# Decode attention with a token mixer: mixer tiles that go on without a pause, one activation for a half's exponentials, V alternating with the next K

## Chip, cores, metric

One core of one Trainium2 chip runs one program. The metric is the device time of one execution in microseconds, the median of three runs; lower is better.

## What is computed

Two inputs of one token (512 channels) go through attention over a long cache, a token mixer, attention again with the same cache and weights, and the mixer again. Each step adds to its input and starts with a layer norm.

```python
def A(x, k_cache, v_cache, wq, wo):            # 32 query heads, 8 heads of K and V, 32768 keys of 128
    q = split_heads(x @ wq)                    # B=2, 32, 1, 128
    scores = q @ repeat(k_cache, 4).T * 128 ** -0.5
    return (softmax(scores) @ repeat(v_cache, 4)).merge_heads() @ wo

def M(x, w1, b1, w2, b2):                      # one token, F=1792
    u = gelu(layernorm(x)[b, s, d] * w1[s, f] + b1[f])      # b, d, f
    return (u @ w2 + b2)                       # b, s, d

x = x + A(layernorm(x)); x = x + M(layernorm(x)); x = x + A(layernorm(x)); x = x + M(layernorm(x))
```

All numbers are float32. K and V of one head and one input are 16 MB each.

## The kernel before

The work is cut into 32 *units*: a layer, an input b and a head of K and V. `units` (L188 on) lists them: the first layer's twelve units of the six "passing" heads, then the ones of heads 5 and 7, in which the layers are interleaved so that one input's mixer runs while the other input still streams its cache. Unit 13 is the last of input 0 in the first layer (`N1`), unit 16 that of input 1 (`N2`), unit 18 is `N3`. Unit 14 and unit 17 are the ones "between layers": while their K chunks are streamed, the mixer of unit 13's (16's) input is computed, and the q of unit 15 (18) needs that mixer's result. Head 7 is the "keeper": of unit 13's and 16's K and V some chunks stay in SBUF and are used again by units 15 and 18. Of K those are chunks 2, 4 and 5 (`KEPT_K`).

A unit has 8 chunks of K and 8 of V, of 2 MB. `stream` lists all chunks with a sort key; the final loop walks it, issues a load on SP's queue (`load_k`, `load_v`) and records the chunk's matmuls (`k_chunk`, L307, 16 matmuls of 128x512 into the PSUM tile `scores`; `v_chunk`, L417, 16 into `acc`). `t` counts chunks. Loads of the other units take up to 8 MB; from unit 14's third K chunk to unit 18 they take 2 MB, into a ring of three buffers (`RING`): a load waits for the chunk that was in its buffer. All other work hangs on that count: `at(t, f, ...)` puts `f` behind the t-th chunk; within one count, lower `rank` comes first, then the order of the `at` calls. Engines run their instructions in the order in which they were recorded.

For a unit the steps are: `make_q` in three parts (two of the projection, L250, one of turning the row into a column, L262); `max_1` and `max_2` (the maximum over all scores, through DVE and PE, to `neg`, L337); `turn_scores` (a DVE transpose from PSUM into S0 or S1, one half of the chunks each); `exponentials` (four activations with an accumulated sum for each half, L346); `denominators`; after the last V chunk `out_1`, `out_2`. The mixer is `mix_1`, `mix_2` (layer norm to `slope` and `shift`), 14 times `hidden_tile` (a gelu activation of 128x512, L640) and `hidden_out` (its matmul, L629), then `take_rows`, `mix_4`, `to_columns`. Between layers its tiles lie in S0, S1 and one tile `hid`, which are free until the unit's scores are turned into S0 and S1; `BURSTS` says how many tiles are made at each count from `begin` on:

```python
BURSTS = (3, 3, 3, 3, 0, 1, 1)
when = [(begin + k, place) for k, m in enumerate(BURSTS) for place in (*S, None)[-m:] if m]
for f, (w, place) in enumerate(when):
    at(w + 1, hidden_out, key, f, rank=0)
    at(w, hidden_tile, key, f, place, rank=2)
```

So three tiles are made behind a K chunk and multiplied behind the next one, four times over; then come the exponentials of unit 14 (17), and the last two tiles follow, one behind each of the first two V chunks. The V chunks 0 to 5 of unit 14 (17) follow one another, and then K of unit 15 (18) and V take turns: the key of V chunk c is `(n + 1) * NCH - 0.5 + max(c / (2 * NCH) - 0.5, c - ASIDE + 1)`, with `ASIDE = 6`.

Of the kernel before, what the change touches and what calls it, by code (L numbers as in the profile page):

```python
# [9 lines left out]
AF = mybir.ActivationFunctionType  # L10
ALU = mybir.AluOpType
AX = mybir.AxisListType

P = 128
# [10 lines left out]
KEPT_K = {2: 9, 4: 7, 5: 8}  # L25
KEPT = {1: (8, 6), 3: (8, 11), 4: (3, 13), 5: (8, 3), 6: (8, 4), 7: (8, 5)}
REST = 3
ASIDE = 6
BURSTS = (3, 3, 3, 3, 0, 1, 1)
KEPT_Q = 4  # L30
RESIDENT = (5, 7)
PIECES = (32, 16, 8, 4, 4)
# [8 lines left out]
def gqa_mixer_kernel(ctx: ExitStack, tc: tile.TileContext, x, kt, v, wqo, cols, out):  # L41
# [17 lines left out]
    nc = tc.nc  # L59
# [3 lines left out]
    NCH = kt.shape[1] // (CK * DH)  # L63
    HKV = U // B
    R = wqo.shape[2] // (2 * D)
    DT = D // P
    FT = (cols.shape[1] - 1) // 3
# [3 lines left out]
    HALVES = NCH // PACK  # L71
    SCALE = DH ** -0.5
# [88 lines left out]
    S = [const.tile([P, 512], F32, name=f"S{k}") for k in range(HALVES)]  # L161
# [34 lines left out]
    N3 = len(units) - 1  # L196
# [9 lines left out]
    def row_tile():  # L206

        return S[HALVES - 1]
# [16 lines left out]
    def unit_of(n):  # L225

        return units[n]
# [47 lines left out]
    sc_ps, mx, lsum, oT = {}, {}, {}, {}  # L275
# [55 lines left out]
    neg = {}  # L331
# [11 lines left out]
    def exponentials(n, half):  # L343
        s = S[half].rearrange("p (t h) -> p t h", h=R)
        for h in range(R):
            nc.scalar.activation(  # L346
                s[:, :, h],
                s[:, :, h],
                AF.Exp,
                bias=neg[n][:, h : h + 1],  # L350
                scale=SCALE,
                accum_out=lsum[n][:, half, h : h + 1],
            )

    def stays(n, c):
# [327 lines left out]
    for n in range(NU):  # L683
        stream += [(n * NCH + c + m - 1, 0, n, c, m, limit) for c, m, limit in parts(n, 0)]
        for c, m, limit in parts(n, 1):
            if n in (N1, N2):
                key = (n + 1) * NCH + 1 + (c + 1) / (2 * NCH)
            elif n in (N1 + 1, N2 + 1):
                key = (n + 1) * NCH - 0.5 + max(c / (2 * NCH) - 0.5, c - ASIDE + 1)
            else:  # L690
                key = (n + 1) * NCH + c + m - 1 + (LAG if N1 < n <= N3 else 0)
# [4 lines left out]
    kbeg, k_done, vbeg, v_done, t = {}, {}, {}, {}, 0  # L696
# [7 lines left out]
    def at(time, f, *a, rank=1):  # L704
        done.setdefault(time, []).append((rank, f, a))
# [5 lines left out]
    for n in range(NU):  # L711
        layer, b, h = unit_of(n)
        kend, vend = k_done[n, NCH - 1], v_done[n, NCH - 1]
        ahead = v_done[n - 1, NCH - 1] if n else 0
        urgent = n in (N1, N2, NU - 1)
        if n:
            if n in (N1 + 2, N2 + 2):
                q0 = q1 = mixed[layer - 1, b]
            else:
                q0 = kbeg[n] - 6  # L720
                q1 = q0 + 1
            q2 = q1 + 1
            assert q2 <= kbeg[n]
            at(q0, make_q, n, 0)
            at(q1, make_q, n, 1)
            at(q2, make_q, n, 2)
        if n and (units[n] == (0, 0, h) or h in passing and units[n] == (1, 0, h)):
            at(kbeg[n] - 10, load_weights, h, (again if layer else weight_cell)[h])
        if n in (N1 + 1, N2 + 1):
            t1 = kend  # L730
            at(kend, max_1, n, 0)
            at(kend, max_2, n)
            at(kend, exponentials, n, 0)
        else:
            t1 = max(kend + 2, ahead + (2 if urgent else 4))
            at(kend + 1, max_1, n)
            at(kend + 2, max_2, n)
            at(max(k_done[n, HC - 1], v_done[n - 1, HC - 1] if n else 0), turn_scores, n, 0)
            at(kend + 2, exponentials, n, 0)
        at(t1, turn_scores, n, 1)  # L740
        at(t1, exponentials, n, 1)
        at(t1 + (1 if n == NU - 1 else 2), denominators, n)
        if n == NU - 1:
            at(t1 + 1, gelu_table)
            at(t1 + 1, last_rows, (layer, b))
            at(vend, last_out, n)
            at(vend, last_mixer, n)
            continue
        assert vbeg[n + 1] >= vend and (n + 2 >= NU or vbeg[n + 1] > vend)
        at(min(vend + 1, vbeg[n + 1]), out_1, n)  # L750
        change = n in (N1, N2)
        at(vend + (1 if change else 2), out_2, n)
        if units[n] == lay[layer, b][-1]:
            key = (layer, b)
            begin = vend + (2 if change else 3)
            at(vend, mix_1, key)
            at(begin - 1, take_rows, key, row_tile())
            at(begin, mix_2, key)
            at(vend + 1, gelu_table)
            if change:  # L760
                assert vend + 5 < k_done[n + 1, NCH - 1] == begin + 4 and sum(BURSTS) == FT
                when = [(begin + k, place) for k, m in enumerate(BURSTS) for place in (*S, None)[-m:] if m]
                e = begin + len(BURSTS)
            else:

                exps = [k_done[m, NCH - 1] + 2 for m in (n + 1, n + 2)]
                exps += [max(e, v_done[m, NCH - 1] + 4) for e, m in zip(exps, (n, n + 1))]
                when = [(w, None) for w in range(begin, begin + FT + 1 + len(exps)) if w not in exps][: FT + 1]
                e = when.pop()[0]

            for f, (w, place) in enumerate(when):
                at(w + 1, hidden_out, key, f, rank=0)
                at(w, hidden_tile, key, f, place, rank=2)
            at(e, take_rows, key, None, rank=2)
            at(e + 1, mix_4, key)
            if layer + 1 < LAYERS:
                at(e + 2, to_columns, key)
                mixed[key] = e + 2
# [9 lines left out]
    t = 0  # L788
# [62 lines left out]
```

## Time and profile before

| | |
|---|---|
| time, median of 3 runs | 2511.01 us (2510.29 to 2512.43) |
| time of the profiled execution | 2509.4 us |
| its span, first to last instruction | 2507.6 us |
| granted TensorE clock, mean | 0.77 |
| busy: PE, DVE, ACT | 55%, 8%, 8% of the span |
| read from HBM | 1068.00 MB, 426 GB/s over the span |

The profile is of one execution. In its tables the engines are PE (TensorE matmul), PEld (its weight load), DVE (VectorE), ACT (ScalarE), POOL (GpSimd) and SP (SyncE, which issues the loads); L417 is line 417 of the kernel. A row of the timeline has start, duration, engine, line, operation, tiles, count, and in brackets the idle time before it with what ended that. A row of busy time by stretch has, for each engine, busy time and number of instructions, then the granted TensorE clock, the share of the 16 DMA engines that was busy, and GB/s.

### The profile page before, as it was taken

The page shows a single profiled execution, that of the slowest core. Times are in us where ns is not written, and L with a number is a line of the kernel's source. Part 1 is how long each engine was busy: PE and PEld are TensorE (multiplying, and loading weights), DVE is VectorE, ACT ScalarE, POOL GpSimd, SP SyncE. Part 2 cuts the span into 40 slices and gives each one's busy share as a digit, 9 for nine tenths or more (in the row PEclk, how much of TensorE's full clock was granted, in tenths as well). Part 3 has the DMA queues.
Part 4 walks back from the last instruction along what each step waited for, and adds up shares of the span by engine and source line. Part 5 has one row for each costly group of instructions (what it writes and reads, how often), then busy time and mean ns, then how long its engine had stood idle before and what let it go on. Part 6 is the DMA issues. An engine that isn't in the chain of part 4 may idle for free.

```text
span 2507.6 us, 20418 instructions
## 1 busy us (share of the span) xinstructions
PE 1382.3 (55%) x9302; PEld 365.0 (15%) x9302; DVE 207.2 (8%) x587; ACT 197.3 (8%) x582; POOL 4.9 (0%) x17
## 2 busy tenths in 40 slices
PE   4545554545445554666676766454546555455546
PEld 1111111111111111111111211111111111111112
DVE  1000000000000000001101100000000000010002
ACT  0000000000000000002012010000000000011102
POOL 0000000000000000000000000000000000000000
PEclk8777777777777777878897987777778777777778
DMA  9999999999999999999999999999999999999996
GB/s 419 433 433 431 433 434 432 433 429 434 433 433 433 431 426 433 424 427 418 427 427 428 408 428 434 433 432 434 431 432 430 433 434 432 431 432 432 430 433 282
DMA packets 31200, 1069.32 MB, mean 426 GB/s; under 512 B 3717, under 2 KB 3721, under 8 KB 4362
## 3 DMA queue, kind: packets, MB, share of 16 engines
q1 hardware_dynamic: 30824, 1067.99, 99.0%
q8 instruction: 73, 1.20, 0.2%
q14 instruction: 13, 0.11, 0.0%
q10 hardware_dynamic: 290, 0.03, 0.0%
HBM read 1068.00 MB, written 0.00 MB: 426 GB/s over the span
## 4 chain that ended last, share of the span: by engine, by line
DMA 74%; PE 25%; ACT 0%; DVE 0%; issue 0%; ACTq 0%; SPq 0%; DVEq 0%
DMA mem<-in_kt_dram 37%; DMA mem<-in_v_dram 37%; PE acc L417 11%; PE scores L307 11%; PE misc L250 1%; PE rows L461 0%; PE misc L454 0%; PE rows L629 0%; PE misc L335 0%; ACT S L346 0%; ACT mem L614 0%; PE misc L446 0%; PE misc L215 0%; PE misc L262 0%; PE misc L327 0%
## 5 line engine op out<-in xcount | busy, mean ns | idle before, releaser
L307 PE MATMUL scores<-mem,qpad 128*32 128x512 f32 x4096 | 616.4, 721 | 594.3 <-DMA mem<-in_kt_dram 593.6
L417 PE MATMUL acc<-mem,S 128*16 128x512 f32 x4088 | 618.3, 743 | 481.0 <-DMA mem<-in_v_dram 473.6
L346 ACT ACTIVATE S<-S,neg 128x128 f32<-128x128 f32 x256 | 132.3, 521 | 2080.0 <-DVE neg L337 1603.8
L307 PEld LDWEIGHTS scores<-mem,qpad 128*32 128x32 f32 x4096 | 142.3, 127 | 981.3 <-DMA mem<-in_kt_dram 525.1
L417 PEld LDWEIGHTS acc<-mem,S 128*16 128x16 f32 x4088 | 134.8, 111 | 850.7 <-issue 697.9
L317 DVE TENSOR_REDUCE mx<-scores 128x1 f32<-128x512 f32 x64 | 44.3, 692 | 854.3 <-PE scores L307 854.3
L250 PE MATMUL misc<-mem,xnT 128*2 128x512 f32 (+1 forms) x144 | 69.6, 611 | 2.8 <-issue 1.8
L341 DVE STREAM_TRANSPOSE S<-scores 128x512 f32<-128x512 f32 x64 | 45.5, 711 | 143.9 <-PE acc L417 143.2
L346 ACT ACTIVATION_READ_ACCUMULATOR S<-S,neg 128x1 f32 x256 | 47.9, 187 | 0.0
L461 PE MATMUL rows<-mem,oT 128*1 128x512 f32 x248 | 33.8, 592 | 0.5 <-DVE oT L456 0.5
L385 DVE SCALAR_TENSOR_TENSOR S<-acc,mask,S 128x128 f32<-128x128 f32 x93 | 32.6, 351 | 3.3
L329 DVE TENSOR_REDUCE m<-misc 1x4 f32<-1x128 f32 x32 | 8.8, 276 | 275.9 <-PE misc L327 275.9
L448 DVE RECIPROCAL rl<-misc 128x4 f32<-128x4 f32 x32 | 5.9, 183 | 307.2 <-PE misc L446 307.2
L629 PE MATMUL rows<-hid,cols_sb 128*1 128x512 f32 x52 | 28.2, 625 | 2.4 <-ACT hid L640 2.4
L262 PE MATMUL misc<-ident,hid 2*128 2x2 f32 (+1 forms) x144 | 19.0, 249 | 19.0 <-DVE hid L259 19.0
L456 DVE TENSOR_TENSOR oT<-misc,rl 128x4 f32<-128x4 f32 x31 | 5.0, 163 | 293.4 <-PE misc L454 293.4
L640 ACT ACTIVATE hid<-bcast,bias,scale 128x512 f32<-128x512 f32 x26 | 20.3, 779 | 78.3 <-PE rows L629 57.9
L383 DVE TENSOR_SCALAR S<-acc,mask 128x128 f32<-128x128 f32 x31 | 10.9, 350 | 168.6 <-PE acc L417 168.6
L262 PEld LDWEIGHTS misc<-ident,hid 2*128 2x128 f32 (+1 forms) x144 | 17.4, 187 | 35.1 <-DVE hid L259 31.7
L640 ACT ACTIVATE S<-bcast,bias,scale 128x512 f32<-128x512 f32 x16 | 11.6, 777 | 111.5 <-DVE bias L512 99.8
L250 PEld LDWEIGHTS misc<-mem,xnT 128*2 128x2 f32 (+1 forms) x144 | 12.1, 86 | 52.0 <-issue 50.9
L454 PEld LDWEIGHTS misc<-selh,S 128*128 128x128 f32 x62 | 12.5, 252 | 44.7 <-issue 43.0
(116 smaller groups left out, 244.9 us busy)
## 6 DMA issues: line engine op xcount, KB each, us to landing
mem<-in_kt_dram SPq DMA_DIRECT2D x44, 2048.0 KB, 12.7
mem<-in_v_dram SPq DMA_DIRECT2D x35, 2048.0 KB, 13.2
mem<-in_v_dram SPq DMA_DIRECT2D x9, 4096.0 KB, 32.7
mem<-in_wqo_dram SPq DMA_DIRECT2D x14, 2048.0 KB, 33.5
mem<-in_kt_dram SPq DMA_DIRECT2D x7, 4096.0 KB, 27.5
mem<-in_v_dram SPq DMA_DIRECT2D x4, 1280.0 KB, 22.6
mem<-in_v_dram SPq DMA_DIRECT2D x2, 768.0 KB, 23.2
mem<-in_v_dram SPq DMA_DIRECT2D x1, 1024.0 KB, 27.8
```

Source lines behind the costliest of these rows:

```text
L250: nc.tensor.matmul(q_ps[n][:m, :], xnT[layer][:, d, b : b + m], wq_at(h)[:, d, :], start=(d == 0), stop=(d == DT - 1),)
L262: nc.tensor.matmul(pt[:, r * m : (r + 1) * m], q_row[n][:m, r * DH : (r + 1) * DH], ident[:m, :m], start=True, stop=True,)
L307: nc.tensor.matmul(sc_ps[n, half][32 * g : 32 * g + 32, :], q, kc[:, (k * NG + g) * w : (k * NG + g + 1) * w], start=(i == 0 and k == 0), ...
L317: nc.vector.tensor_reduce(mx[n][:, half : half + 1], sc_ps[n, half], axis=AX.X, op=ALU.max)
L341: nc.vector.transpose(S[half], sc_ps[n, half])
L346: nc.scalar.activation(s[:, :, h], s[:, :, h], AF.Exp, bias=neg[n][:, h : h + 1], scale=SCALE, accum_out=lsum[n][:, half, h : h + 1],)
L385: nc.vector.scalar_tensor_tensor(t, acc[:, k * DH : (k + 1) * DH], mask[:, k : k + 1], t, op0=ALU.mult, op1=ALU.add)
L417: nc.tensor.matmul(acc[32 * g : 32 * g + R * QT, :], S[half][:, col : col + R * QT], (own if q < stay else vc)[:, q * w : (q + 1) * w], st ...
L454: nc.tensor.matmul(po[:, :R], asb, selh, start=True, stop=True)
L461: nc.tensor.matmul(rows[b][32 * r : 32 * r + 1, :], oT[n][:, r : r + 1], wo_at(h)[:, r, :], start=(units[n] == lay[layer, b][0]), stop=(un ...
L629: nc.tensor.matmul(rows[key[1]][32 * g : 32 * g + 1, :], w2c[:, f : f + 1], hid[key, f], start=(f < NG), stop=(f >= FT - NG),)
L640: nc.scalar.activation(hid[key, f], px[key], AF.Gelu_apprx_tanh, bias=shift[key][:, f : f + 1], scale=slope[key][:, f : f + 1],)
```

## The change

Four things change, all around units 14 and 17 but for the last.

- The mixer's tiles between layers go through three places in turn (`hid`, S1, S0). Three tiles are made ahead; from then on each `hidden_out` is followed by the `hidden_tile` that fills the same place. All 14 are made and multiplied before the unit's exponentials, and the mixer's last steps move two or three counts earlier.
- The exponentials of these two units are made by a DVE pass that scales and adds `neg`, one activation for a half, and later one DVE sum for a half.
- `ASIDE` is 3: after V chunks 0 to 2 of unit 14 (17), K chunks of unit 15 (18) and V chunks take turns.
- The projection of q for unit 19 (`N3 + 1`) starts 10 counts ahead of its K, not 6.

```diff
-ASIDE = 6
-BURSTS = (3, 3, 3, 3, 0, 1, 1)
+ASIDE = 3
+BURSTS = (0, 4, 4, 4, 2)
...
+    def exponentials_at_once(n, half):
+        s = S[half].rearrange("p (t h) -> p t h", h=R)
+        nc.vector.scalar_tensor_tensor(
+            s, s, SCALE, neg[n].unsqueeze(1).to_broadcast([P, P, R]), op0=ALU.mult, op1=ALU.add
+        )
+        nc.scalar.activation(S[half], S[half], AF.Exp)
+
+    def sums(n):
+        for half in range(HALVES):
+            nc.vector.tensor_reduce(
+                lsum[n][:, half, :], S[half].rearrange("p (t h) -> p h t", h=R), axis=AX.X, op=ALU.add
+            )
...
-                q0 = kbeg[n] - 6
+                q0 = kbeg[n] - (10 if n == N3 + 1 else 6)
...
             at(kend, max_1, n, 0)
             at(kend, max_2, n)
-            at(kend, exponentials, n, 0)
+            at(kend, exponentials_at_once, n, 0)
+            at(kend, turn_scores, n, 1)
+            at(kend, exponentials_at_once, n, 1)
+            at(kend + 1, sums, n)
...
-                when = [(begin + k, place) for k, m in enumerate(BURSTS) for place in (*S, None)[-m:] if m]
-                e = begin + len(BURSTS)
+                places = (None, *reversed(S))
+                through = [begin + k for k, m in enumerate(BURSTS) for _ in range(m)]
+                for f in range(len(places)):
+                    at(begin, hidden_tile, key, f, places[f], rank=2)
+                for f, w in enumerate(through):
+                    at(w, hidden_out, key, f, rank=0)
+                    if f + len(places) < FT:
+                        at(w, hidden_tile, key, f + len(places), places[f % len(places)], rank=0)
+                e = begin + len(BURSTS) - 1
```

At `e` stands `take_rows`, at `e + 1` `mix_4`, at `e + 2` `to_columns` and the first two parts of `make_q` for unit 15 (18), as before. In the order of PE's instructions, V chunk 0 is then followed by `mix_4`, V chunk 1 by `to_columns`, the denominators and the projection, V chunk 2 by q's column.

More of the change, by code (lines that the diff above doesn't have):

```diff
@@ L739, in gqa_mixer_kernel @@
             at(kend + 2, exponentials, n, 0)
-        at(t1, turn_scores, n, 1)
-        at(t1, exponentials, n, 1)
+            at(t1, turn_scores, n, 1)
+            at(t1, exponentials, n, 1)
         at(t1 + (1 if n == NU - 1 else 2), denominators, n)
@@ L760, in gqa_mixer_kernel @@
             if change:
-                assert vend + 5 < k_done[n + 1, NCH - 1] == begin + 4 and sum(BURSTS) == FT
-                when = [(begin + k, place) for k, m in enumerate(BURSTS) for place in (*S, None)[-m:] if m]
-                e = begin + len(BURSTS)
+                assert k_done[n + 1, NCH - 1] == begin + len(BURSTS) - 1 and sum(BURSTS) == FT
+                places = (None, *reversed(S))
[7 more added lines that the diff above has]
+                e = begin + len(BURSTS) - 1
             else:
@@ L767, in gqa_mixer_kernel @@
                 exps += [max(e, v_done[m, NCH - 1] + 4) for e, m in zip(exps, (n, n + 1))]
[L768 to L773, printed above, removed]
+                when = [w for w in range(begin, begin + FT + 1 + len(exps)) if w not in exps][: FT + 1]
+                e = when.pop()
+                for f, w in enumerate(when):
+                    at(w + 1, hidden_out, key, f, rank=0)
+                    at(w, hidden_tile, key, f, rank=2)
             at(e, take_rows, key, None, rank=2)
```

## The prediction

> **What bounds the kernel now.** I read the page first: span, engine shares, the slices and the chain that ended last.
>
> ```profile
> span 2507.6 us, 20418 instructions
> PE 1382.3 (55%) x9302; PEld 365.0 (15%) x9302; DVE 207.2 (8%) x587; ACT 197.3 (8%) x582; POOL 4.9 (0%) x17
> DMA  9999999999999999999999999999999999999996
> GB/s 419 433 433 431 433 434 432 433 429 434 433 433 433 431 426 433 424 427 418 427 427 428 408 428 434 433 432 434 431 432 430 433 434 432 431 432 432 430 433 282
> DMA 74%; PE 25%; ACT 0%; DVE 0%; issue 0%; ACTq 0%; SPq 0%; DVEq 0%
> HBM read 1068.00 MB, written 0.00 MB: 426 GB/s over the span
> ```
>
> No compute engine is above 55%, the DMA digit is 9 in every slice but the last, and the chain is three quarters DMA. The 25% of PE in it is how the chain walks from one load to the chunk whose end frees its buffer; it is no idle time of the DMA. So the time is bytes over rate, plus whatever stretches the DMA engines stand dry. The second view, busy time by stretch, says where that can be.
>
> ```profile
> 50.00:1090.00 1040.00, 540.86 (x3658) 143.21 (x3654) 71.62 (x204) 56.14 (x208) 0.00 (x0) 0.74 1.00 431
> 1090.00:1500.00 410.00, 285.92 (x1856) 71.40 (x1844) 47.61 (x132) 57.41 (x140) 2.17 (x4) 0.86 1.00 423
> 1500.00:2480.00 980.00, 516.33 (x3447) 136.49 (x3448) 71.17 (x203) 74.89 (x227) 0.54 (x1) 0.75 1.00 432
> 2480.00:2507.60 27.60, 19.65 (x259) 8.11 (x258) 10.98 (x28) 7.58 (x8) 0.54 (x1) 0.94 0.25 102
> ```
>
> The last three numbers are granted TensorE clock, DMA share and GB/s. The diff touches only what runs between 1090 and 1500 us: the two change-overs between the layers, units 14 and 17 with their mixers, and the q projection of unit 19. The tail after 2480 is not touched. Even in the stretch of the change the DMA share rounds to 1.00: if all of it ran at the 431 of the stretch ahead, 410 us would shrink by 410 x 8/431 = 7.6 us, and most of that is the rate of its smaller 2 MB loads, which stay. The third view is the same one, narrower, around the mixers.
>
> ```profile
> 1180.00:1190.00 10.00, 9.27 (x53) 2.01 (x52) 0.35 (x2) 5.99 (x12) 0.00 (x0) 0.74 0.96 377
> 1380.00:1385.00 5.00, 4.77 (x40) 1.24 (x33) 0.18 (x1) 2.99 (x4) 0.00 (x0) 1.00 0.90 360
> 1430.00:1440.00 10.00, 9.41 (x88) 3.51 (x89) 1.29 (x4) 0.00 (x0) 0.00 (x0) 1.00 0.85 334
> 1440.00:1450.00 10.00, 4.33 (x32) 1.13 (x28) 1.06 (x3) 2.22 (x9) 0.00 (x0) 0.73 1.01 433
> ```
>
> These three are the dips I find there: two just after a mixer unit's exponentials, one where unit 18 runs chunks of K that are kept in SBUF. That is all the change can win, and it can be priced in three ways. By DMA share: 10 x 0.04 + 5 x 0.10 + 10 x 0.15 = 2.4 us. By bytes against the 433 of the full row: 10 x 56/433 + 5 x 73/433 + 10 x 99/433 = 4.4 us. By landings, from the PE timeline, where a chunk's first matmul starts as its load lands:
>
> ```profile
> 1158.39 1.92 PE L307 MATMUL scores<-mem,qpad 128*32 128x512 f32 x16 [1.92 <-DMA mem<-in_kt_dram]
> 1163.29 1.92 PE L307 MATMUL scores<-mem,qpad 128*32 128x512 f32 x16 [1.21 <-DMA mem<-in_kt_dram]
> 1179.89 6.25 PE L417 MATMUL acc<-mem,S 128*16 128x512 f32 x32 [2.41 <-ACT S L346]
> 1188.04 1.91 PE L417 MATMUL acc<-mem,S 128*16 128x512 f32 x16 [0.73 <-DMA mem<-in_v_dram]
> 1194.13 2.34 PE L417 MATMUL acc<-mem,S 128*16 128x512 f32 x16 [3.33 <-DMA mem<-in_v_dram]
> 1383.31 1.91 PE L417 MATMUL acc<-mem,S 128*16 128x512 f32 x16 [0.23 <-DMA mem<-in_v_dram]
> 1389.07 1.88 PE L417 MATMUL acc<-mem,S 128*16 128x512 f32 x12 [3.01 <-DMA mem<-in_v_dram]
> 1431.31 7.07 PE L307 MATMUL scores<-mem,qpad 128*32 128x512 f32 x64
> 1438.64 1.92 PE L307 MATMUL scores<-mem,qpad 128*32 128x512 f32 x16 [0.25 <-DMA mem<-in_kt_dram]
> 1443.98 3.05 PE L307 MATMUL scores<-mem,qpad 128*32 128x512 f32 x16 [3.25 <-DMA mem<-in_kt_dram]
> ```
>
> The beat is 1163.29 - 1158.39 = 4.90 us for a 2 MB load. The three late landings are 6.09, 5.76 and 5.34 us after the one ahead: 1.19 + 0.86 + 0.44 = 2.5 us. Two ways agree near 2.4; the bytes give the upper bound, 4.4. The lower bound is nothing: the share is a mean over 16 engines, and a load has landed when the last of them is done. Where only engines that were ahead ran dry, filling the dip moves no end.
>
> **The change part by part.** (1) *One activation for a half's exponentials.* For units 14 and 17, four activations and their accumulator reads become a DVE pass over 128x512 (scale, add), one activation, and later one DVE sum per half.
>
> ```profile
> 1177.71 0.53 ACT L346 ACTIVATE S<-S,neg 128x128 f32<-128x128 f32 x1 [1.49 <-DVE neg L337]
> 1181.89 1.28 ACT L640 ACT_TABLE_LOAD   x1
> L385 DVE SCALAR_TENSOR_TENSOR S<-acc,mask,S 128x128 f32<-128x128 f32 x93 | 32.6, 351 | 3.3
> L341 DVE STREAM_TRANSPOSE S<-scores 128x512 f32<-128x512 f32 x64 | 45.5, 711 | 143.9 <-PE acc L417 143.2
> L640 ACT ACTIVATE hid<-bcast,bias,scale 128x512 f32<-128x512 f32 x26 | 20.3, 779 | 78.3 <-PE rows L629 57.9
> L317 DVE TENSOR_REDUCE mx<-scores 128x1 f32<-128x512 f32 x64 | 44.3, 692 | 854.3 <-PE scores L307 854.3
> ```
>
> On the path today lie the four activations, from 1177.71 to the first V matmul at 1179.89: 2.18 us. The new pass does not stand in the trace: its size costs 0.71 (the transpose of 128x512), its operation 4 x 0.351 = 1.40. I take 0.71, since a quarter of the elements at four times the fixed part overstates it. With 0.78 for the activation the path is 1.49 us (1.40 would give 2.18, no gain): 0.7 us earlier. The second half's pass and activation, the copy of the mixer's row and the two sums (0.69 each) stand behind it on DVE and ACT, and hide beside the first V chunk, which PE multiplies without them; the denominators wait for the sums, a chunk or more later. The sums cost the path nothing unless DVE is more than a chunk late.
>
> (2) *All mixer tiles before the exponentials.* The fourteen tiles go through hid, S1, S0 in turn; a tile is refilled as soon as its matmul has read it. Tiles 12 and 13, which lay among the V chunks with a table load on either side of each pair, move ahead: two of four switches per mixer go, 1.28 us each on an ACT that nobody waits for there. Each K chunk now has four tile matmuls behind it, not three, one of which waits for a tile made in the same step: an activation of 0.78 us within the 4.90 - 1.92 = 3.0 us that PE has spare per chunk at full clock. I cost it at nothing; the cover is that spare time. Without it a buffer comes free about 1 us late, and the two loads still queued hide that.
>
> (3) *What the first V buffer's release does.* SP issues loads in order, each waiting for the chunk three loads back.
>
> ```profile
> 1183.57 0.33 SPq L374 DMA_DIRECT2D mem<-in_v_dram  x1
> 1436.73 0.33 SPq L292 DMA_DIRECT2D mem<-in_kt_dram  x1
> 1180.00:1185.00 5.00, 5.00 (x27) 0.85 (x28) 0.16 (x1) 3.93 (x10) 0.00 (x0) 0.50 1.00 383
> ```
>
> The issue at 1183.57 is the load behind the first V chunk, whose matmuls ran at clock 0.50. With (1) it comes some 0.7 us earlier, as a K load of unit 15. That takes most, not all, of the first two dips: 0.9 us by share, of which I count 0.6.
>
> (4) *V alternates with the next K.* The same loads, same bytes, another order: after three V chunks, K of unit 15 (18) and V of unit 14 (17) take turns. The kept K chunks 2, 4 and 5, which need no load, then stand one at a time between loaded chunks. Today chunks 4 to 7 make the unbroken run of 64 matmuls at 1431.31, with unit 19's projection and unit 17's output just ahead of it; SP's load behind it went out only at 1436.73, as the queue was emptying. (Unit 15 has the same kept chunks, but its neighbour's q was kept aside and needs no projection there; I find no dip.) In the new order each pair of loads has one kept chunk beside it, and the projection of unit 19 stands four steps earlier. I count the third dip as gone, 1.5 us by share, less 0.1 for what may remain: 1.4.
>
> (5) *The price.* The chain from mixer to unit 15's q is moved up to behind V chunks 0 to 2: copy, mixer output, columns, projection, q. Queued behind its matmuls on PE is V chunk 2, whose release lets SP issue K chunk 1.
>
> ```profile
> 1200.87 1.05 PE L215 MATMUL misc<-ident,hid 128*128 128x1 f32 x8
> 1202.42 3.16 PE L250 MATMUL misc<-mem,xnT 128*1 128x512 f32 x7 [0.50 <-DVE xnT L221]
> 1205.00:1210.00 5.00, 4.75 (x39) 1.92 (x41) 0.84 (x2) 0.00 (x0) 0.00 (x0) 1.00 1.00 429
> ```
>
> Count from chunk 1's landing, L: its matmuls 1.9, columns 1.05, about 1 for DVE and two short matmuls, projection 3.2 and a bit, say 3.4, chunk 2's 1.9: released at L + 9.3. The load must land at L + 4 x 4.90 = 19.6; issued to a nearly dry queue it took 1443.98 - 1436.73 = 7.25 us, so it must go out by L + 12.4. Slack 3.1 us: nothing lost at full clock.
>
> The sum is 0.6 + 1.4 = 2.0 us. The profiled execution took 2509.4 (span 2507.6 and 1.8 around it), 1.6 below the median of 2511.0; taken off the span it gives 2505.6, off the median **2509.0 us**. A measurement of this kernel tells about 0.2% (5.0 us) from no change, so this is "same".
>
> **Rivals.** *A: the dips were free.* Only engines that ran ahead were dry; the late landings of 1.19 and 0.86 have another cause. For it: the share in the narrow row is 1.00 in 1180 to 1185, when the queue was at its thinnest. Against it: 0.85 in the third dip. Result 2511.0, within 1 us.
>
> *B: slower, at half clock.* Point (5) rests on the granted clock. At 0.50, as in 1180 to 1185, its 8.2 us of matmuls take 16.4; with the 1 us beside them chunk 2 is released at L + 17.4, 5.0 us past the last moment. Two change-overs lose 10, the 2.0 of gain goes against it: 2519. It decides where the 8.2 us stretch past 11.4, at a mean clock under 0.72; at 0.63 each change-over loses 1.6 us, and with no gain left that is 2514. Against it: this work, where it stands today, ran at 1.00 (1205 to 1210). For it: it will follow the wait for the exponentials more closely, and behind that wait of 2.41 us the clock was 0.50. "TensorE: Matmul & The Clock Gate" in the Trainium skill (Part 1) says that the array falls to half rate after an idle window of about 3.4 us and comes back after a busy one of that length; by that rule V chunks that wait for their loads would bring B about, and the time would be B's. This trace agrees in part: half rate came behind a wait shorter than that window.
>
> *C: faster by over 5 us.* It needs all 4.4 us of the bytes and a lucky run as well: about 2506 or below.
>
> **How the numbers follow.** Forecast (gain 1 to 4.4) 0.60, A 0.24, B 0.11, C 0.05. Only B leaves "same" upward, and not all of it (the half-way clock above stays within 5 us): slower 0.09; faster 0.05; same 0.86. Range: 2511.0 - 4.4 and 0.7 of scatter below (the runs reach from 2510.3 to 2512.4) give 2505.9; above, A with that scatter is 2512.4, and B at the half-way clock is 2514. That leaves out C and the upper part of B.
>
> **What would show it.** Right: the share in the stretches behind the two mixers and in unit 18's kept chunks back to 1.00 with some 430 GB/s; landings on the 4.90 beat; the first V matmul 1.5 us, not 2.2, behind neg; two table loads fewer per mixer. Wrong: a new row under 0.95 where V and K take turns, an SP load behind V chunk 2 issued over 12 us after chunk 1 landed, or a DVE pass of 1.4 us. If the landings keep the beat and the time does not move, A holds.

## The result and the profile after

| | before | after |
|---|---|---|
| median of 22 runs each | 2512.18 us (2507.45 to 2514.66) | 2506.98 us (2506.42 to 2508.12) |
| ratio | | 0.9983, 95% interval 0.9976 to 0.9989 |
| profiled execution, its span | 2509.4, 2507.6 us | 2506.78, 2505.0 us |

The change makes the kernel faster by 0.17%, which on 2512 us is 4.3 us (2.8 to 6.0 by the interval). It also makes it steadier: the runs of before spread over 7.2 us, those of after over 1.7. The medians lie 5.2 us apart, the two profiled executions only 2.6: the profile on which the prediction rests was one of the cheaper runs of before.

The page of after: span, engines, slices, chain.

```profile
span 2505.0 us, 20394 instructions
PE 1392.4 (56%) x9302; PEld 365.6 (15%) x9302; DVE 213.1 (9%) x595; ACT 185.3 (7%) x550; POOL 4.9 (0%) x17
GB/s 419 434 433 432 434 431 431 434 433 436 434 429 429 435 433 430 428 422 423 424 427 426 420 429 433 434 433 430 436 433 428 435 433 431 434 434 431 430 432 285
DMA 74%; PE 24%; DVE 1%; issue 0%; ACT 0%; ACTq 0%; SPq 0%; DVEq 0%
```

The bound is the same, DMA. The lowest inner slice of before, 408 GB/s (the 23rd, from 1379 us on), is 420 now. The same stretches as in the prediction, busy time by stretch:

```profile
1090.00:1500.00 410.00, 286.01 (x1855) 70.30 (x1847) 53.63 (x140) 46.66 (x110) 2.17 (x4) 0.87 1.00 424
1180.00:1190.00 10.00, 8.72 (x42) 2.63 (x35) 4.12 (x10) 0.00 (x0) 0.54 (x1) 0.87 1.00 403
1380.00:1385.00 5.00, 3.72 (x22) 1.64 (x15) 2.83 (x8) 0.00 (x0) 0.54 (x1) 0.90 0.99 416
1385.00:1390.00 5.00, 5.00 (x21) 0.81 (x20) 0.68 (x1) 0.00 (x0) 0.00 (x0) 0.76 0.92 393
1390.00:1395.00 5.00, 4.69 (x41) 1.75 (x40) 0.16 (x1) 0.00 (x0) 0.00 (x0) 1.00 0.91 364
1430.00:1440.00 10.00, 4.83 (x40) 1.22 (x36) 0.85 (x2) 0.00 (x0) 0.00 (x0) 0.93 1.00 426
1500.00:2480.00 980.00, 524.46 (x3464) 138.73 (x3468) 71.66 (x203) 73.87 (x223) 0.54 (x1) 0.75 1.00 432
```

In the rows of the prediction all three dips are filled: 0.96, 0.90 and 0.85 have become 1.00, 0.99 and 1.00. But between 1385 and 1395 us, where V and K now take turns, the share is 0.92 and 0.91, and it was 1.02 in both rows of before: the second dip has moved rather than gone. In the third dip PE is half idle where it was 94% busy. The timeline of PE there, and SP's K loads of after and, below them, of before (a row stretches from the first of its four issues to the end of the last):

```profile
1428.25 1.92 PE L307 MATMUL scores<-mem,qpad 128*32 128x512 f32 x16 [0.94 <-DMA mem<-in_kt_dram]
1433.14 1.92 PE L307 MATMUL scores<-mem,qpad 128*32 128x512 f32 x16 [2.11 <-DMA mem<-in_kt_dram]
1438.13 3.27 PE L307 MATMUL scores<-mem,qpad 128*32 128x512 f32 x16 [3.06 <-DMA mem<-in_kt_dram]
1442.94 1.92 PE L307 MATMUL scores<-mem,qpad 128*32 128x512 f32 x16 [1.21 <-DMA mem<-in_kt_dram]
1416.19 14.37 SPq L292 DMA_DIRECT2D mem<-in_kt_dram  x4
```

```profile
1416.62 20.44 SPq L292 DMA_DIRECT2D mem<-in_kt_dram  x4
```

Every chunk now waits for its load, and the loads land on the beat of 4.90 us. The last of the four loads goes out by 1430.56 instead of 1437.06, 6.5 us earlier. So far the forecast's mechanism. What it is worth, and which of the four edits brings it, only runs can tell.

### The profile page after: what moved, and what is told of

Read it like the earlier page. It is cut to its first block, busy times and chain, and to the rows that moved or that the text cites. A ratio compares the mean times of both kernels' runs of the same rounds, so it can differ in the third digit from the quotient of the medians.

```text
span 2505.0 us, 20394 instructions
## 1 busy us (share of the span) xinstructions
PE 1392.4 (56%) x9302; PEld 365.6 (15%) x9302; DVE 213.1 (9%) x595; ACT 185.3 (7%) x550; POOL 4.9 (0%) x17
## 4 chain that ended last, share of the span: by engine, by line
DMA 74%; PE 24%; DVE 1%; issue 0%; ACT 0%; ACTq 0%; SPq 0%; DVEq 0%
DMA mem<-in_kt_dram 38%; DMA mem<-in_v_dram 36%; PE acc L431 11%; PE scores L307 11%; PE misc L250 1%; PE rows L475 0%; PE misc L468 0%; PE misc L335 0%; PE misc L460 0%; ACT mem L628 0%; DVE lsum L365 0%; PE rows L643 0%; PE bcast L666 0%; PE misc L327 0%; ACT mem L617 0%
## 5 line engine op out<-in xcount | busy, mean ns | idle before, releaser
L307 PE MATMUL scores<-mem,qpad 128*32 128x512 f32 x4096 | 627.2, 732 | 593.8 <-DMA mem<-in_kt_dram 593.1
L346 ACT ACTIVATE S<-S,neg 128x128 f32<-128x128 f32 x240 | 123.4, 517 | 2088.1 <-DVE neg L337 1612.8
L327 PE MATMUL misc<-ident,mxa 128*1 128x128 f32 x64 | 16.8, 355 | 0.3 <-DVE mxa L323 0.3
```

What stands on the lines that cost most here:

```text
L307: nc.tensor.matmul(sc_ps[n, half][32 * g : 32 * g + 32, :], q, kc[:, (k * NG + g) * w : (k * NG + g + 1) * w], start=(i == 0 and k == 0), ...
L327: nc.tensor.matmul(pm[:1, :P], mxa, ident, start=True, stop=True)
L346: nc.scalar.activation(s[:, :, h], s[:, :, h], AF.Exp, bias=neg[n][:, h : h + 1], scale=SCALE, accum_out=lsum[n][:, half, h : h + 1],)
```

## The experiments

The theory (W): the whole gain is the third dip, by the early q of unit 19 or by the alternation (which of the two was left open), and the tiles and exponentials are worth nothing. Its rivals: the gain is in the first two dips, from the tiles and exponentials; or no dip is worth anything and the difference lies elsewhere. Times of e1 to e7 are medians of eleven runs, ratios are against before on the same chip (2511.65 us beside e1 to e4, 2510.27 beside e5 to e7).

**e1, the early q alone**, put into the kernel before:

```diff
-                q0 = kbeg[n] - 6
+                q0 = kbeg[n] - (10 if n == N3 + 1 else 6)
```

> The kernel before with one edit: the projection of q for unit 19 starts 10 counts ahead of its K, not 6. Theory W (the third dip, where unit 18's kept K chunks run without a pause, is most of the 4.3 us that the change gained, and it is a loss that varies from run to run, which is why the kernel before spreads over 7 us and the changed one over 2): the stretch loses its longest guest, the time falls by 2 to 4 us and the spread of the runs narrows. Rival F (the two dips behind the mixers carry it): at most 1 us faster, spread as before.

Measured: 2507.04 us (2506.55 to 2511.1), ratio 0.9985 (0.9976 to 0.9994): the whole gain in the median, from one line. Three of the eleven runs are slower, 2509.02 to 2511.1 us, and none of those was profiled; of the 22 runs of after none is above 2508.12. Two stretches and the PE timeline of e1:

```profile
1180.00:1190.00 10.00, 8.68 (x54) 1.97 (x54) 0.35 (x2) 7.12 (x16) 0.00 (x0) 0.83 0.85 351
1430.00:1440.00 10.00, 5.75 (x54) 1.38 (x46) 0.85 (x2) 0.00 (x0) 0.00 (x0) 1.00 1.01 429
1426.47 5.33 PE L307 MATMUL scores<-mem,qpad 128*32 128x512 f32 x48
```

The first dip is deeper than in before (0.85 against 0.96) and e1 is as fast as after, in its profile too (2506.74). The third is gone: with the projection out of the way the run of kept K is 48 matmuls and ends at 1431.8, where before's 64 ended at 1438.4.

**e2, after without the alternation**, and **e3, after without the early q:**

```diff
-ASIDE = 3
+ASIDE = 6
```

> The changed kernel with ASIDE back at 6: six V chunks ahead, then K and V by turns; tiles, exponentials and the early q stay. Theory W by way of the alternation: the unbroken run of kept chunks is back, 2 to 4 us slower than the changed kernel, and the spread returns. W by way of the early q: within 1 us of the changed kernel. Rival F: within 1 us of the changed kernel, and as narrow.

```diff
-                q0 = kbeg[n] - (10 if n == N3 + 1 else 6)
+                q0 = kbeg[n] - 6
```

> The changed kernel with unit 19's q back at 6 counts ahead. Theory W by way of the alternation: within 1 us of the changed kernel. W by way of the early q: 2 to 4 us slower. Rival F: within 1 us.

Measured: e2 2506.89 us, ratio 0.9979 (0.9970 to 0.9988); e3 2507.18 us, ratio 0.9986 (0.9977 to 0.9995). Neither median can be told from that of after. Each of the two edits can go, as long as the other stays. The profiled execution of e3 was its slowest, 2509.68, and shows something else, at the second change-over:

```profile
1390.00:1395.00 5.00, 4.75 (x38) 1.80 (x34) 0.84 (x2) 0.00 (x0) 0.00 (x0) 0.98 0.80 298
1430.00:1440.00 10.00, 6.44 (x58) 1.60 (x50) 2.25 (x7) 0.00 (x0) 0.00 (x0) 1.00 0.99 424
1385.56 4.86 PE L250 MATMUL misc<-mem,xnT 128*1 128x512 f32 x7
1392.65 0.33 SPq L292 DMA_DIRECT2D mem<-in_kt_dram  x1
```

The third dip is not there, but one stands at 1390: the projection took 4.86 us, and the load behind V chunk 2 went out at 1392.65. I come back to it under the price.

**e4, after with the old exponentials** (four activations for a half, no DVE sums):

```diff
-            at(kend, exponentials_at_once, n, 0)
+            at(kend, exponentials, n, 0)
...
-            at(kend, exponentials_at_once, n, 1)
-            at(kend + 1, sums, n)
+            at(kend, exponentials, n, 1)
```

> The changed kernel with the four activations for a half and their accumulated sums back in units 14 and 17, in place of the DVE pass, one activation and the later sums. Theory W: within 1 us of the changed kernel; the first V matmul of these units 0.6 to 0.7 us later, the load behind it too, and no dip that moves the end. Rival F: the two dips behind the mixers come back, 2 to 3 us slower than the changed kernel and a spread of 5 us.

Measured: 2507.35 us (2506.71 to 2508.93), ratio 0.9984 (0.9975 to 0.9993). The single activation for a half is worth at most some tenths of a microsecond, which these runs cannot tell from nothing. The steps came near what was expected: at the first mixer the first V matmul starts 0.57 us later than in after (1179.15), and the load behind it goes out 1.10 us later (1182.83).

**e5, after without the early q and without the alternation**; the tiles and the exponentials stay:

```diff
-ASIDE = 3
+ASIDE = 6
...
-                q0 = kbeg[n] - (10 if n == N3 + 1 else 6)
+                q0 = kbeg[n] - 6
```

> The changed kernel with both the early q and the alternation undone (q 6 counts ahead, ASIDE 6); tiles and exponentials stay as changed. If the third dip is all of the gain: as slow as the kernel before, within 1 us (a ratio of 0.9996 to 1.0004), with its spread of 6 us or so, and the dip in the stretch of unit 18's kept chunks. If tiles and exponentials carry a share of their own: 1 to 2 us faster than before.

Measured: 2512.91 us (2509.75 to 2515.33), ratio 1.0008 (0.9999 to 1.0017). All gain is gone and the spread of before is back, with the first dip filled. It is slower than before by 2.0 us by the ratio, not within the 1 us expected; the interval reaches from 0.3 us faster to 4.3 slower, so these runs do not tell whether the tiles and exponentials cost something while the third dip is open:

```profile
1180.00:1190.00 10.00, 8.35 (x50) 2.78 (x50) 4.39 (x11) 0.00 (x0) 0.55 (x1) 1.00 0.99 421
1430.00:1440.00 10.00, 8.84 (x78) 3.20 (x80) 2.01 (x4) 0.00 (x0) 0.00 (x0) 1.00 0.76 290
```

e1 and e5 together decide between W and the first rival: first dip open and third filled is fast, first filled and third open is slow.

**e6, a try at a better version:** without the alternation, and the two sums behind the columns on DVE, since in after they stand ahead of them:

```diff
-ASIDE = 3
+ASIDE = 6
...
-            at(kend + 1, sums, n)
+            at(kend + 3, sums, n)
...
-        at(t1 + (1 if n == NU - 1 else 2), denominators, n)
+        at(t1 + (1 if n == NU - 1 else 4 if n in (N1 + 1, N2 + 1) else 2), denominators, n)
```

> The fastest of the kernels so far (the changed one with ASIDE 6), with the two DVE sums moved behind the mixer's columns and the denominators two counts later, so that the columns no longer wait 0.75 us for the sums. Theory W: the DMA has no dip left here that moves the end, so nothing is gained: within 0.3 us of 2506.9. A rival (what waits on PE still costs): 0.5 to 1 us faster.

Measured: 2506.77 us (2506.22 to 2508.77), ratio 0.9980 (0.9972 to 0.9989). The timelines of after and then of e6, the chain from the mixer's columns to xT:

```profile
1184.85 2.00 DVE L365 TENSOR_REDUCE lsum<-S 128x4 f32<-128x512 f32 x2
1184.97 1.05 PE L215 MATMUL misc<-ident,hid 128*128 128x1 f32 x8
1186.77 0.21 DVE L219 TENSOR_SCALAR xT<-misc,cols_sb 128x4 f32<-128x4 f32 x1
```

```profile
1184.79 1.05 PE L215 MATMUL misc<-ident,hid 128*128 128x1 f32 x8
1185.88 0.22 DVE L219 TENSOR_SCALAR xT<-misc,cols_sb 128x4 f32<-128x4 f32 x1 [1.12 <-PE misc L215]
1186.20 2.02 DVE L365 TENSOR_REDUCE lsum<-S 128x4 f32<-128x512 f32 x2
```

In after xT comes 0.75 us behind PE's last column (1186.02), in e6 at once. The chain is shorter and the time is that of after and e2: what this chain releases is hidden.

**e7, before with unit 19's projection doubled:** four more matmuls in each half, with a column of zeros as weights, so that they take PE's time and add nothing.

```diff
+                for _ in range(n == N3 + 1 and 0 < d < DT - 1 and 2):
+                    nc.tensor.matmul(
+                        q_ps[n][:m, :], zero[:, :m], wq_at(h)[:, d, :], start=False, stop=False
+                    )
```

> The kernel before with the projection of q for unit 19 made twice as long: four more matmuls of the same shape with zeros as weights, which add nothing to q, 3.4 us of PE at full clock, in the stretch of unit 18's kept chunks. Theory W: PE sets the pace there, so the DMA stands dry 2 to 3.4 us longer and the time grows by 2 to 4 us over the kernel before. Rival F: no slower than before, within 0.5 us.

Measured: 2514.58 us (2512.52 to 2516.81), ratio 1.0011 (1.0002 to 1.0020), and 2516.2 in the profiled execution. Busy time by stretch, and SP's four K loads, the last of which is out at 1444.39, 7.3 us later than in before:

```profile
1430.00:1440.00 10.00, 8.84 (x58) 2.82 (x60) 2.04 (x4) 0.00 (x0) 0.00 (x0) 0.90 0.62 241
1440.00:1450.00 10.00, 7.64 (x66) 2.17 (x58) 1.13 (x3) 0.00 (x0) 0.00 (x0) 0.93 0.56 211
1416.70 27.69 SPq L298 DMA_DIRECT2D mem<-in_kt_dram  x4
```

More PE work at this one place costs time. It lies on the path, as W says.

**b1 to b4, a2: before profiled four times more, after once.** The first was to see whether the dip of the first profile is a typical one, the others whether the spread of before comes from it. No edit.

> The kernel before once more, for a second profile of it. Theory W: where its time is above 2509.4 us, the dip in the stretch of unit 18's kept chunks is deeper than 1.5 us by share, by as much as the time is longer, and the dips behind the mixers differ without that; where its time is below, it is shallower. Rival F: the dips behind the mixers follow the time.

> The kernel before, profiled again, to see whether its spread comes from the third dip. Theory W (the time above 2506.8 us is what unit 18's late landings cost): two landings between 1430 and 1450 us come later than the 4.90 beat by an excess E, and the time is 2506.8 + E + 0 to 3 us; the DMA share of 1430 to 1450 is the lower, the slower the run. Rival (the spread of 7 us has another source, the dip is always worth the same): E is 0.5 to 1.7 us, as in the two profiles shown so far, whatever the time is.

> As for the run ahead: W: time = 2506.8 + E + 0 to 3 us. Rival: E of 0.5 to 1.7 us at any time from 2507 to 2515 us.

> As for the run ahead: W: time = 2506.8 + E + 0 to 3 us. Rival: E of 0.5 to 1.7 us at any time from 2507 to 2515 us.

> The kernel after, profiled again. W: landings on the beat through 1430 to 1450 us, share 1.00, 2506.4 to 2508.1 us. Rival: the same time, with a share under 0.95 there in some of the profiles.

The stretch from 1430 to 1440 us in b1, b2, b3, b4, in this order, then the unbroken run of 80 matmuls of b1 and of b3 and the chunk behind it of b3, from the PE timelines, one stretch inside b3's run, and last the V chunk that stands ahead of the projection in before and in b3:

```profile
1430.00:1440.00 10.00, 8.84 (x81) 3.33 (x84) 1.99 (x5) 0.00 (x0) 0.00 (x0) 1.00 0.72 269
1430.00:1440.00 10.00, 8.84 (x62) 2.94 (x58) 2.04 (x4) 0.00 (x0) 0.00 (x0) 0.83 0.66 256
1430.00:1440.00 10.00, 8.84 (x62) 2.94 (x58) 2.04 (x4) 0.00 (x0) 0.00 (x0) 0.83 0.62 239
1430.00:1440.00 10.00, 8.84 (x65) 3.19 (x68) 1.49 (x4) 0.00 (x0) 0.00 (x0) 0.83 0.60 234
1432.51 8.79 PE L307 MATMUL scores<-mem,qpad 128*32 128x512 f32 x80
1433.60 10.49 PE L307 MATMUL scores<-mem,qpad 128*32 128x512 f32 x80
1447.82 0.88 PE L307 MATMUL scores<-mem,qpad 128*32 128x512 f32 x4 [3.54 <-DMA mem<-in_kt_dram]
1434.42:1437.84 3.42, 3.42 (x20) 0.87 (x16) 0.00 (x0) 0.00 (x0) 0.00 (x0) 0.50 0.73 311
1419.15 1.91 PE L417 MATMUL acc<-mem,S 128*16 128x512 f32 x16 [2.58 <-DMA mem<-in_v_dram]
1418.77 3.61 PE L417 MATMUL acc<-mem,S 128*16 128x512 f32 x16 [3.02 <-DMA mem<-in_v_dram]
```

The column to read is the granted clock: 1.00, then three times 0.83. The run of kept K takes 8.79 us at the one and 10.49 at the other; the 1.7 us between them are one stretch of 3.42 us at half clock. The rest of the difference lies ahead of the run: the V chunk takes 1.91 us in before and 3.00 to 3.61 in b1 to b4 and e5, and the run starts 1.1 to 2.4 us later than in before. So one and the same kernel has a shallow dip or a deep one.

The table sets the times beside the landings, which I read from the events of the loads' semaphores. E is how much longer than two beats (9.80 us) the two loads take that land last in this dip; F is how much later than the beat another load lands, near 1475 us in before (later in the slower profiles, 1482 in e7).

| kernel | time, us | share 1430 to 1440 | E, us | F, us | time above 2506.8 |
|---|---|---|---|---|---|
| after, a2, e1 | 2506.78, 2506.66, 2506.74 | 1.00 to 1.01 | 0.0 | 0.0, 0.3, 0.1 | 0.0, -0.1, -0.1 |
| before | 2509.4 | 0.85 | 0.5 | 1.25 | 2.6 |
| b1 | 2510.22 | 0.72 | 1.6 | 1.4 | 3.4 |
| e5 | 2510.39 | 0.76 | 1.7 | 1.3 | 3.6 |
| b4 | 2512.46 | 0.60 | 3.8 | 1.5 | 5.7 |
| b2 | 2512.72 | 0.66 | 4.7 | 1.35 | 5.9 |
| b3 | 2514.27 | 0.62 | 4.7 | 1.4 | 7.5 |
| e7 | 2516.2 | 0.62, 0.56 | 8.3 | 1.2 | 9.4 |

W holds: the time is 2506.8 + E and 1.1 to 2.8 us more (0 to 3 were expected), of which F is 1.2 to 1.5. The rival, E of 0.5 to 1.7 whatever the time, is refuted by three of the profiles. E follows SP's last K load: against before it goes out 1.2 us later in b1, 1.6 in e5, 2.8 in b4, 4.1 in b2, 4.0 in b3 and 7.3 in e7, and E is 1.1, 1.2, 3.3, 4.2, 4.2 and 7.8 us more. The first dip does not follow the time: from 1180 to 1190 us the share is 0.87, 0.99, 1.00 and 0.88 in b1 to b4, and b3, which is the slowest, has none there. The profiles near the median of before, 2512 (b4, b2), have a deep third dip; the profile that the prediction had is the one with the shallowest of the five.

## Why the prediction was right, and where it was not

The median, 2506.98, lies in the range, and 0.17% is within the 0.2% that the prediction called "same". The gain was 2.0 us by the sum and 4.3 by the ratio. That the range holds the median is partly luck: its lower end took 4.4 us for all three dips from the bytes of one execution, and the gain came from the third dip alone, which is deeper in most executions than in that one. By its steps:

- **What bounds the kernel:** right. The DMA, and dips between 1090 and 1500 us; 1500 to 2480 us runs at 432 GB/s as before.
- **(1) One activation:** its durations were right but for the sums. Three groups of after, and the timeline at the first mixer:

```profile
L365 DVE TENSOR_REDUCE lsum<-S 128x4 f32<-128x512 f32 x4 | 4.0, 1040 | 0.0
L358 DVE SCALAR_TENSOR_TENSOR S<-S,neg 128x512 f32<-128x512 f32 x4 | 2.8, 692 | 0.1
L361 ACT ACTIVATE S<-S 128x512 f32<-128x512 f32 x4 | 2.5, 630 | 8.9 <-DVE S L358 8.9
```

```profile
1177.17 0.69 DVE L358 SCALAR_TENSOR_TENSOR S<-S,neg 128x512 f32<-128x512 f32 x1
1177.90 0.63 ACT L361 ACTIVATE S<-S 128x512 f32<-128x512 f32 x1 [3.73 <-DVE S L358]
1178.58 3.10 PE L431 MATMUL acc<-mem,S 128*16 128x512 f32 x16 [1.64 <-ACT S L361]
1181.73 0.33 SPq L292 DMA_DIRECT2D mem<-in_kt_dram  x1
```

  The pass took 0.69 us (0.71 taken, 1.40 the other bound), the activation 0.63 (0.78 taken), and the first V matmul starts 1.41 us after the pass (2.18 after the first activation in before): the 0.7 of the working. A sum took 1.04, not 0.69; it reads every fourth element, which may be why, but no run tests it. The two stood ahead of the columns on DVE and held them up 0.75 us, for which e6 shows no price.
- **(2) The tiles,** costed at nothing: right, within what e5 can tell: they are in e5, which gains nothing.
- **(3) The first two dips, 0.6 us:** this term failed. The first closes as foreseen (the load behind the first V chunk now goes out 4.56 us behind the start of the pass, where it was 5.86 behind the first activation), the second moves, and neither is worth anything measurable: e1 has the first one open and is as fast as after, and e5 has both places filled (0.99, and 1.00 from 1380 to 1390 us) and is no faster than before. For these two dips rival A was right, and by the landings for its reason. The late landing of 1.19 us near 1194, on which the price by landings rested, has another cause (a candidate stands in the last section): in after, with the share at 1.00, a landing at 1193.4 is still 0.88 late, in a2 1.20, in e2 1.53.
- **(4) The third dip, 1.4 us:** the mechanism was right (SP's load behind the unbroken run of kept K goes out as the queue empties) and the size was wrong. In the profiles of before it is worth 2.6 to 7.5 us, if all that lies above 2506.8 is put down to E and what follows it. The working took one execution's dip for the kernel's, and in that execution the V chunk ahead of the run and the run itself went at full clock. It also counted both edits together. Either does it: e1 and e3 reach the whole gain in the median, each with one of them, and the second one has next to nothing left to gain.
- **(5) The price, nothing:** right for after, with much less slack than the 3.1 us of the working. At the second change-over of after:

```profile
1378.58 1.91 PE L431 MATMUL acc<-mem,S 128*16 128x512 f32 x16
1383.06 4.86 PE L250 MATMUL misc<-mem,xnT 128*1 128x512 f32 x7
1390.15 0.33 SPq L292 DMA_DIRECT2D mem<-in_kt_dram  x1
1378.50:1390.00 11.50, 10.22 (x51) 2.82 (x51) 4.80 (x11) 0.00 (x0) 0.54 (x1) 0.85 0.97 406
```

  Chunk 1 landed at 1378.34, so the load behind V chunk 2 went out at L + 11.8, not L + 9.3: 1.7 us are the projection at a lower clock (4.86 us at 0.65, against the 3.16 of before), most of the rest DVE's sums. It still landed on the beat (1397.89, 4.91 us behind the one ahead). In e3's profile the same load went out at L + 12.2 (1392.65 behind 1380.48) and landed 1.57 us late, at 1401.79: rival B's mechanism, once, in a profile in which the third dip was absent. So the last moment lies, as far as these two executions tell, between 11.8 and 12.2, earlier than the 12.4 of the working, and after stands just inside it. Rival B asked for a mean clock under 0.72; here 0.85 (the last row) was nearly enough, with the sums in front. One of the prediction's signs of being wrong, a row under 0.95 where V and K take turns, did come (0.91 from 1390 us on), without a late landing there in after.
- **Rival B's 2519 us** did not come: the V chunks that wait for their loads did not bring half clock over all of step (5). Slow matmuls did follow some waits: the 16 of a K chunk took 3.27 us at 1438.13, behind 3.06 us of idle, and those at 1178.58 took 3.10 behind 1.64, while the ones at 1433.14 took 1.92 behind 2.11. "TensorE: Matmul & The Clock Gate" in the Trainium skill (Part 1) gives an idle window of about 3.4 us for the fall to half rate; these runs agree that waits can bring slow matmuls, but they came behind shorter waits, and not in the order of their length.

## What to carry to other kernels

Where loads wait in one queue for buffers, look for the place where most of the engine's work stands in an unbroken run without a load of its own: what that run holds back is priced by when its end lets the next load go, and a step of 3 us moved out of it can be worth more than a rebuilt stage. A dip in the DMA share is a lead, not a price; close one dip and leave the others open, in both ways, before they are added up. And profile the kernel before several times: its best run and its worst were 7 us apart, and in its five profiles the time went with this one place, so one trace could tell the mechanism but not the size.

## What was not expected of the hardware

- **The same run of 80 matmuls took 8.79 or 10.49 us,** at a granted clock of 1.00 or 0.83, in executions of one kernel. Start and length of the run make up the delay of SP's last load: in b1 and e5 the run only starts later than in before, by 1.2 and 1.6 us, and E is 1.6 and 1.7; in b4, b3 and b2 it starts 1.1, 2.3 and 2.4 us late and is 1.7 longer, and E is 3.8, 4.7 and 4.7. The same 1.70 us stand between the projection's 3.16 and 4.86 and between the V chunk's 1.91 and 3.61. What decides whether the clock falls there was not tested.
- **A dip goes on costing after it is over.** A load's semaphore has 16 events in the trace, one for each engine's part, and the chunk's first matmul waits for the last. In after and e1 the first and the last part of a load lie 2.0 to 3.5 us apart around 1440 to 1480 us. In all seven profiles with the third dip this shrinks there, from 1.9 to 3.6 us ahead of it to 0.3 to 0.6 behind it: the engines that were ahead have waited for the others. Near 1475 a load then lands 1.2 to 1.5 us late (F) and the parts lie 1.6 to 1.8 apart again, as if one engine had been held up; none of the profiles without the dip has that landing late by more than 0.3. So a lead of some engines seems to absorb later delays of single ones, and a dip uses it up. It would also say why the first two dips are free, where only leads were lost. That is read from the landings; no run held up one engine on purpose.
- **Packets of a second queue go with the late landings.** The DMA queues of before from 1466 to 1478 us, packets, MB and share of 16 engines:

```profile
q8 instruction: 1, 0.02, 0.6%
```

  By its name in the profile this queue fetches instructions: 73 packets of 16 KB in the whole span of before. In all seven profiles with the third dip one of them, 1.02 to 1.09 us long, starts 2.6 to 2.7 us ahead of the landing that is late by F, and there one of the load's 16 parts alone is late. In after, a2 and e1 it starts at 1471.3 to 1471.6 us, and no landing is more than 0.3 late behind it. Such a packet also starts 2.0 to 4.4 us ahead of the late landing near 1194 in thirteen of the fourteen profiles (all but e4), and 2.1 us ahead of the one that is 0.86 late at 1389 in before. So the landings by which the prediction priced the first two dips go with these packets, dip or no dip. That is a reading of times; no run moved a packet.
- **Open:** what is left of the times in the table after E and F, -0.2 to 1.4 us, the profile of e4 (2508.93, without a third dip, with single landings late by 1.71 at 1198.8 and 1.36 at 1278.6), the landing late by 1.53 at 1302.0 in e3's profile, and the three slow runs of e1.
